# POOL writes its products into the mixed tile itself, and two buffers go

## The chip, the cores and the metric

The kernel runs on one core of a Trainium2 chip. The metric is the device time of one execution in microseconds (us). The core's engines are TensorE (PE, matrix products), VectorE (DVE), ScalarE (ACT), GpSimd (POOL) and SyncE (SP, which here issues the transfers). Each runs its own list of instructions in order; semaphores make one wait for another.

## The reference

Three layers stand behind each other: attention over keys near each query and over 24 block summaries, a channel mixer gated by a sigmoid, and a token and channel mixer. There are 2 sequences of 768 rows with 512 channels (8 heads of 64). The change is in the second layer:

```python
def _moe_ref(x, mu_k, mu_r, w_k, w_v, w_r) -> np.ndarray:
    B, S, D = x.shape
    x_prev = np.concatenate([np.zeros((B, 1, D), dtype=np.float32), x[:, :-1, :]], axis=1)
    xk = mu_k * x + (1.0 - mu_k) * x_prev
    xr = mu_r * x + (1.0 - mu_r) * x_prev
    k = np.maximum(xk @ w_k, 0.0)
    v = k * k @ w_v
    r = 1.0 / (1.0 + np.exp(-(xr @ w_r)))
    return (r * v).astype(np.float32)
```

Its input x is the attention's output. Each row is mixed with the row before it, once with the weights mu_k for the branch through w_k and w_v, and once with mu_r for the gate through w_r. The third layer follows on the result: `h = np.maximum(xt @ w_tok1, 0.0) @ w_tok2` over the tokens, then `(u + np.maximum(u @ w_ch1, 0.0) @ w_ch2)` over the channels.

## The kernel before, in words

**Numbers in two parts.** Matrix products of the second and third layer are made three times, from a high part and a low part of each operand (hi*hi, hi*lo, lo*hi; `mm3`, L432). ACT copies a tile to its high part, and POOL or DVE subtracts that from the tile for the low part.

**Attention.** 24 units (2 sequences, 6 tiles of 128 queries, 2 halves of the heads) go through scores on PE (sp, L303), mask and minimum on DVE (sm, L309), exponential on ACT (pe, L312), division by the sum on POOL (pe, L322), transposition on PE (pt, L328) with a copy to PT, the product with the values on PE (pv, L345), and a copy by ACT into xT (L350). xT holds the activations with the channels on the partitions. Block summaries are written by POOL into kw (L229).

**The mixed tiles.** `mixed` (L417 to L425) takes 256 rows and all 512 channels, in four slices of 128 channels (d). For each slice POOL multiplies the rows shifted by one with 1 - mu into a tile tmp (L421), from a tag with two buffers, and DVE adds mu times the rows and writes slice d of the tile xk (L422). xk has one buffer. When the four slices are done, ACT copies xk to the high part xh (L423) and DVE subtracts for the low part xl (L424); xh and xl have two buffers each. Six mixed tiles feed the branch (`main`), six the gate (`gate_pass`), and `main` makes one of the gate's tiles a second time, so that 13 are made: 52 products and 52 updates.

**The branch and the gate.** `main` makes, for each mixed tile, four groups of 24 matmuls into a bank ko. `k2_tile` squares the positive part: rl on ACT (L444) and DVE (L445), high part kh on ACT (L446), low part kl on POOL (L447). While the next group runs, the group before is multiplied with w_v into acc (12 matmuls). The gate's products go into ro (24 matmuls for each mixed tile), and a sigmoid on ACT and a product on DVE (L605) put them into ybuf. Then come h (L432, token mixing, 18 matmuls each), gh and gl (the two parts of its positive part, L660 and L661), ho, and the channel mixing (go and o).

**The weights.** They come in 64 bits; ACT, DVE (L145, L149, L155), ACT (high part w, L157) and POOL (low part w, L158) turn each block of 128 x 512 into two parts. Two wf buffers lie between DVE and POOL.

**The order.** The code is written as generators that hand out work in turns (`attention`, `main`, `gate_pass`, weights by credits). A scheduler then sets the order of each engine from estimated durations and priorities; some weight steps are kept in program order. So an edit in one place can move instructions on all engines. SP's list holds transfers only.

**What else uses the two buffers.** Three mask tiles are built at the start in the tag t32, the same tag as tmp.

Of the kernel before, what the change touches and what calls it, by code (L numbers as in the profile page):

```python
# [9 lines left out]
F32 = mybir.dt.float32  # L10
# [4 lines left out]
ALU = mybir.AluOpType  # L15
# [9 lines left out]
MW = 256  # L25
# [26 lines left out]
def fused_kernel(ctx, tc, q, k, v, vt, mu, w_k, w_v, w_r, w_t1, w_t2, w_c1, w_c2, out):  # L52
    nc = tc.nc
# [132 lines left out]
    work = pool("work", "left")  # L186
    xp = pool("xp", "left", reuse_waits="tile")
    XB = S + 1
    xT = xp.tile([128, KD, B * XB], F32, name="xT")
# [224 lines left out]
    def mixed(t0, mu, om):  # L414
        x0 = t0 // S * XB + 1 + t0 % S
        xk = work.tile([128, KD, MW], F32, tag="x32", bufs=1, name="xk")
        hi = work.tile([128, KD, MW], F32R, tag="xh", bufs=XBUFS, name="xh")  # L417
        lo = work.tile([128, KD, MW], F32R, tag="xl", bufs=XBUFS, name="xl")
        for d in range(KD):
            tmp = work.tile([128, MW], F32, tag="t32", bufs=2, name="tmp")  # L420
            nc.gpsimd.tensor_scalar(tmp, xT[:, d, x0 - 1:x0 - 1 + MW], om[:, d:d + 1], 1.0, ALU.mult, ALU.mult)  # L421
            nc.vector.scalar_tensor_tensor(xk[:, d], xT[:, d, x0:x0 + MW], mu[:, d:d + 1], tmp, ALU.mult, ALU.add)  # L422
        nc.scalar.copy(hi, xk)  # L423
        nc.vector.tensor_tensor(lo, xk, hi.bitcast(F32), ALU.subtract)  # L424
        return [(hi[:, d], lo[:, d]) for d in range(KD)]  # L425
# [29 lines left out]
    def make(c):  # L455
        if c not in made and c < NMC and done_tiles[0] >= (c + 1) * MT:
            made[c] = mixed(c * MW, muk, omk)
        elif c not in made and NMC <= c < 2 * NMC and c - NMC in done:
            made[c] = mixed((c - NMC) * MW, mur, omr)
# [73 lines left out]
    masks = []  # L533
    for kind in range(3):
        mc = const.tile([128, NC], F32, name=f"mask{kind}")
        mm = work.tile([128, 2, 128], F32, tag="t32", bufs=2, name="mm")
        for half in range(2):
            m = mm[:, half, :NC]
            nc.gpsimd.memset(m, 0.0)
            first = 64 * half - PAD  # L540
            keys = m[:, NB:NC] if half == 0 else m[:, 0:NK]
            for base, cm, st in ((first + EDGE, -1, 1), (EDGE - first, 1, -1)):
                nc.gpsimd.affine_select(out=keys, in_=keys, pattern=[[st, NK]], compare_op=ALU.is_ge, fill=-8.0 * BIG,
                                        base=base, channel_multiplier=cm)
            if kind == 1 and half == 0:
                nc.gpsimd.memset(m[:, NB:NB + PAD], -8.0 * BIG)
            if kind == 2 and half == 1:
                nc.gpsimd.memset(m[:, NK - PAD:NK], -8.0 * BIG)
            nc.gpsimd.memset(m[:, 0:NB] if half == 0 else m[:, NK:NC], math.sqrt(D) * math.log(BLOCK))
            nc.gpsimd.tensor_scalar(mc[64 * half:64 * half + 64], m[64 * half:64 * half + 64], 1.0, 1.0, ALU.mult, ALU.mult)  # L550
        masks.append(mc)
# [269 lines left out]
```

## Time and profile before

| | |
|---|---|
| three timed runs | 520.34, 521.74, 524.0 us; median 521.74 |
| the profiled execution | its span, from first to last instruction, is 518.7 us; its time beside the span is not given, so the median of the runs stands for it |
| busy time | PE 500.0, DVE 250.7, POOL 205.2, ACT 204.2 us |
| the chain that ended last | PE 80%, POOL 7%, issue 4%, DVE 3%, transfers 2%, ACT 2% |
| granted clock of PE, mean | 0.994 |

A matmul's busy time runs from its start to its modelled end, and successive ones overlap, so a busy PE can still be one that waits a little. The profile's names read "out<-in"; a bracket behind a row gives the idle time of that engine just before, and what ended it.

### The profile page before, as it was taken

How to read it: one execution, taken by the hardware profiler on the slowest of the kernel's cores; microseconds unless marked ns; L12 is line 12 of the kernel's file. 1: busy time of each engine (PE TensorE's matmuls, PEld its weight loads, DVE VectorE, ACT ScalarE, POOL GpSimd, SP SyncE). 2: the span in 40 equal slices, each digit the busy share in tenths (PEclk: the TensorE clock that was granted, in tenths of full speed). 3: DMA queues.
4: the chain of work that ended last, by engine and by line, in shares of the span. 5: the costliest groups of instructions: out<-in, count | busy, mean ns of one | idle time of the engine just before them, and what ended most of it. 6: DMA issues, size and time to landing. Idle time of an engine off the chain costs nothing.

```text
span 518.7 us, 7924 instructions
## 1 busy us (share of the span) xinstructions
PE 500.0 (96%) x2968; PEld 405.6 (78%) x2968; DVE 250.7 (48%) x556; ACT 204.2 (39%) x471; POOL 205.2 (40%) x298
## 2 busy tenths in 40 slices
PE   8997889999999999999999999999999999999995
PEld 3566767888789988888867788888888888888884
DVE  3869998551132667587656766443331211311112
ACT  0668669763342555446345344443211110100100
POOL 6579989972152665388523323322100000000000
PEclk9899999999999999999999999999999999999998
DMA  8999923210066000000176361000020000200002
GB/s 265 322 307 370 313 65 102 67 51 0 1 244 243 1 2 0 1 1 1 42 243 221 145 202 42 1 1 0 1 81 2 0 0 1 81 1 0 1 0 81
DMA packets 24197, 45.40 MB, mean 88 GB/s; under 512 B 2112, under 2 KB 11328, under 8 KB 24160
## 3 DMA queue, kind: packets, MB, share of 16 engines
q1 hardware_dynamic: 24160, 44.90, 26.7%
q8 instruction: 23, 0.38, 0.3%
q14 instruction: 14, 0.11, 0.1%
HBM read 41.16 MB, written 3.15 MB: 85 GB/s over the span
## 4 chain that ended last, share of the span: by engine, by line
PE 80%; POOL 7%; issue 4%; DVE 3%; DMA 2%; ACT 2%; SPq 1%; POOLq 0%; DVEq 0%; ACTq 0%
PE o L746 19%; PE go L432 19%; PE ko L432 11%; PE acc L432 10%; PE ro L432 5%; PE pv L345 3%; PE sp L303 3%; PE ho L432 3%; POOL pe L322 3%; PE h L432 2%; PE pt L328 2%; POOL w L158 2%; PE spin L511 2%; POOL tmp L421 1%; DMA xT<-in_vt_dram 1%
## 5 line engine op out<-in xcount | busy, mean ns | idle before, releaser
L432 PE MATMUL go<-u,w 128*128 128x512 f32 x432 | 106.6, 393 | 0.0
L158 POOL TENSOR_TENSOR w<-wf,w 128x512 fp32r<-128x512 f32 x50 | 65.9, 1320 | 76.9 <-ACT w L157 75.6
L432 PEld LDWEIGHTS go<-u,w 128*128 128x128 f32 x432 | 80.7, 188 | 17.6
L746 PE MATMUL o<-w,gh 128*128 128x512 f32 x288 | 89.0, 395 | 0.0
L661 DVE SCALAR_TENSOR_TENSOR gl<-go,gh 128x512 fp32r<-128x512 f32 x36 | 24.9, 691 | 121.1 <-ACT gh L660 120.9
L432 PE MATMUL ko<-xh,w 128*128 128x256 f32 x384 | 78.1, 289 | 1.6 <-ACT xh L423 0.8
L660 ACT ACTIVATE gh<-go 128x512 fp32r<-128x512 f32 x36 | 21.6, 599 | 128.7 <-PE go L432 128.7
L432 PEld LDWEIGHTS ko<-xh,w 128*128 128x128 f32 x384 | 61.8, 188 | 5.2 <-POOL w L158 1.2
L746 PEld LDWEIGHTS o<-w,gh 128*128 128x128 f32 x288 | 54.0, 188 | 12.0
L432 PE MATMUL acc<-w,kh 128*128 128x512 f32 x192 | 59.8, 401 | 0.7 <-ACT kh L446 0.6
L746 PE MATMUL o<-w,gl 128*128 128x512 f32 x144 | 55.4, 394 | 0.0
L432 PE MATMUL ko<-xl,w 128*128 128x256 f32 x192 | 54.8, 285 | 0.0
L322 POOL TENSOR_SCALAR pe<-pe,den 128x120 f32<-128x120 f32 x96 | 46.2, 499 | 6.7 <-DVE den L320 6.2
L157 ACT CAST w<-wf 128x512 fp32r<-128x512 f32 x50 | 30.9, 618 | 44.7 <-DVE wf L155 42.7
L447 POOL TENSOR_TENSOR kl<-rl,kh 128x512 fp32r<-128x512 f32 x24 | 34.6, 1443 | 34.8 <-ACT kh L446 32.6
L421 POOL TENSOR_SCALAR tmp<-xT,oms 128x256 f32<-128x256 f32 x52 | 34.0, 664 | 33.1 <-DVE xk L422 23.9
L155 DVE SCALAR_TENSOR_TENSOR wf<-wst,wf 128x512 int32<-128x512 int32 x50 | 43.3, 870 | 7.4 <-ACT wst L145 5.7
L312 ACT ACTIVATE pe<-sm,mn 128x120 f32<-128x120 f32 x96 | 37.0, 387 | 22.5 <-DVE mn L309 16.4
L445 DVE TENSOR_TENSOR rl<-rl 128x512 f32<-128x512 f32 x24 | 19.6, 818 | 46.2 <-ACT rl L444 46.2
L432 PEld LDWEIGHTS acc<-w,kh 128*128 128x128 f32 x192 | 34.3, 188 | 8.4 <-ACT kh L446 1.3
L432 PE MATMUL acc<-w,kl 128*128 128x512 f32 x96 | 36.5, 401 | 2.0 <-POOL kl L447 2.0
L422 DVE SCALAR_TENSOR_TENSOR xk<-xT,mus,tmp 128x256 f32<-128x256 f32 x52 | 35.7, 709 | 5.0 <-POOL tmp L421 5.0
(79 smaller groups left out, 722.5 us busy)
## 6 DMA issues: line engine op xcount, KB each, us to landing
wst<-in_moe_w_ch_dram SPq DMA_DIRECT2D x24, 512.0 KB
wst<-in_moe_w_k_dram SPq DMA_DIRECT2D x8, 512.0 KB
wst<-in_moe_w_v_dram SPq DMA_DIRECT2D x8, 512.0 KB
kw<-in_k_dram SPq DMA_DIRECT2D x12, 320.0 KB
wst<-in_moe_w_tok_dram SPq DMA_DIRECT2D x6, 512.0 KB
out_dram<-o SPq DMA_DIRECT2D x12, 256.0 KB
ybuf<-in_v_dram SPq DMA_DIRECT2D x12, 192.0 KB
vw<-in_v_dram SPq DMA_DIRECT2D x12, 192.0 KB
```

The costliest lines, as they stand in the source:

```text
L155: nc.vector.scalar_tensor_tensor(wi, top, 3, wi, ALU.logical_shift_left, ALU.bitwise_or)
L157: self.rounded.append(nc.scalar.copy(hi, wf))
L158: nc.gpsimd.tensor_tensor(lo, wf, hi.bitcast(F32), ALU.subtract)
L312: nc.scalar.activation(pe, s, AF.Exp, bias=mn[:, p:p + 1], scale=-1.0, accum_out=den[:, p:p + 1])
L322: nc.gpsimd.tensor_scalar(z["P"][p], z["P"][p], den[:, p:p + 1], 1.0, ALU.mult, ALU.mult)
L421: nc.gpsimd.tensor_scalar(tmp, xT[:, d, x0 - 1:x0 - 1 + MW], om[:, d:d + 1], 1.0, ALU.mult, ALU.mult)
L422: nc.vector.scalar_tensor_tensor(xk[:, d], xT[:, d, x0:x0 + MW], mu[:, d:d + 1], tmp, ALU.mult, ALU.add)
L432: nc.tensor.matmul(o, l, r, start=(first and i == 0), stop=(last and i == 3 * n - 1))
L447: nc.gpsimd.tensor_tensor(lo, rl, hi.bitcast(F32), ALU.subtract)
L660: nc.scalar.activation(hi, o, AF.Relu)
L661: nc.vector.scalar_tensor_tensor(lo, o, 0.0, hi.bitcast(F32), ALU.max, ALU.subtract)
L746: nc.tensor.matmul(acc[t], l, r, start=(f == 0 and i == 0), stop=(f == nf - 1 and i == 2))
```

## The change

POOL's product of slice d goes into slice d of xk, and DVE reads that slice and overwrites it. tmp is gone, and with it the two buffers of 256 columns; the masks are built in the tag rl, which has two larger buffers. The instructions are the same in number and shape. One line fewer moves the line numbers behind it by one.

```diff
@@ -417,9 +417,8 @@
         hi = work.tile([128, KD, MW], F32R, tag="xh", bufs=XBUFS, name="xh")
         lo = work.tile([128, KD, MW], F32R, tag="xl", bufs=XBUFS, name="xl")
         for d in range(KD):
-            tmp = work.tile([128, MW], F32, tag="t32", bufs=2, name="tmp")
-            nc.gpsimd.tensor_scalar(tmp, xT[:, d, x0 - 1:x0 - 1 + MW], om[:, d:d + 1], 1.0, ALU.mult, ALU.mult)
-            nc.vector.scalar_tensor_tensor(xk[:, d], xT[:, d, x0:x0 + MW], mu[:, d:d + 1], tmp, ALU.mult, ALU.add)
+            nc.gpsimd.tensor_scalar(xk[:, d], xT[:, d, x0 - 1:x0 - 1 + MW], om[:, d:d + 1], 1.0, ALU.mult, ALU.mult)
+            nc.vector.scalar_tensor_tensor(xk[:, d], xT[:, d, x0:x0 + MW], mu[:, d:d + 1], xk[:, d], ALU.mult, ALU.add)
         nc.scalar.copy(hi, xk)
         nc.vector.tensor_tensor(lo, xk, hi.bitcast(F32), ALU.subtract)
         return [(hi[:, d], lo[:, d]) for d in range(KD)]
@@ -533,7 +532,7 @@
     masks = []
     for kind in range(3):
         mc = const.tile([128, NC], F32, name=f"mask{kind}")
-        mm = work.tile([128, 2, 128], F32, tag="t32", bufs=2, name="mm")
+        mm = work.tile([128, 2, 128], F32, tag="rl", bufs=2, name="mm")
         for half in range(2):
             m = mm[:, half, :NC]
             nc.gpsimd.memset(m, 0.0)
```

The scheduler puts the instructions of PE, ACT, DVE and POOL in another order from the first mixed tile on; on SP two loads move. PE's last 945 of 2570 rows are the same. Three places follow.

On POOL, from the second mixed tile of the branch to the second kl, before:

```order
L158 TENSOR_TENSOR w<-wf,w 128x512
L421 TENSOR_SCALAR tmp<-xT,oms 128x256 x2
L322 TENSOR_SCALAR pe<-pe,den 128x120 x4
L158 TENSOR_TENSOR w<-wf,w 128x512
L421 TENSOR_SCALAR tmp<-xT,oms 128x256 x2
L158 TENSOR_TENSOR w<-wf,w 128x512
L322 TENSOR_SCALAR pe<-pe,den 128x120 x4
L447 TENSOR_TENSOR kl<-rl,kh 128x512
L158 TENSOR_TENSOR w<-wf,w 128x512
L229 TENSOR_SCALAR kw<-ks 128x4x24 x12
L158 TENSOR_TENSOR w<-wf,w 128x512
L447 TENSOR_TENSOR kl<-rl,kh 128x512
```

POOL at the same place now:

```order
L322 TENSOR_SCALAR pe<-pe,den 128x120 x4
L158 TENSOR_TENSOR w<-wf,w 128x512
L420 TENSOR_SCALAR xk<-xT,oms 128x256 x4
L322 TENSOR_SCALAR pe<-pe,den 128x120 x4
L158 TENSOR_TENSOR w<-wf,w 128x512
L446 TENSOR_TENSOR kl<-rl,kh 128x512
L158 TENSOR_TENSOR w<-wf,w 128x512
L229 TENSOR_SCALAR kw<-ks 128x4x24 x12
L446 TENSOR_TENSOR kl<-rl,kh 128x512
L158 TENSOR_TENSOR w<-wf,w 128x512 x3
```

The four products stand in one run; the first kl is behind the w that followed it, and the next w is ahead of the twelve kw.

On PE, where the first kl is used (the first acc of the branch, while the second sequence's attention begins; vp transposes the values' sums), before:

```order
L432 MATMUL acc<-w,kh 128x512 x4
L432 MATMUL acc<-w,kl 128x512 x2
L432 MATMUL acc<-w,kh 128x512 x2
L432 MATMUL acc<-w,kl 128x512
L432 MATMUL acc<-w,kh 128x512 x2
L432 MATMUL acc<-w,kl 128x512
L252 MATMUL vp<-ident,vrs 24x128
L328 MATMUL pt<-ident,pe 120x128 x4
L252 MATMUL vp<-ident,vrs 24x128
L303 MATMUL sp<-kw,qT 64x120 x15
L432 MATMUL ko<-xh,w 128x256
L432 MATMUL ko<-xl,w 128x256
```

PE at the same place now:

```order
L431 MATMUL acc<-w,kh 128x512 x4
L252 MATMUL vp<-ident,vrs 24x128
L328 MATMUL pt<-ident,pe 120x128 x4
L252 MATMUL vp<-ident,vrs 24x128
L431 MATMUL acc<-w,kl 128x512 x2
L431 MATMUL acc<-w,kh 128x512 x2
L431 MATMUL acc<-w,kl 128x512
L431 MATMUL acc<-w,kh 128x512 x2
L431 MATMUL acc<-w,kl 128x512
L431 MATMUL ko<-xh,w 128x256
L431 MATMUL ko<-xl,w 128x256
```

The vp and pt have moved ahead of the first acc with kl; the ko stand ahead of the sp.

On PE at the end of the gate: the last mixed tile's ro and the first two h, before:

```order
L432 MATMUL acc<-w,kl 128x512
L432 MATMUL ro<-w,xh 128x512 x4
L432 MATMUL h_3281<-y,w 128x512 x18
L432 MATMUL ro<-w,xl 128x512
L432 MATMUL ro<-w,xh 128x512 x2
L432 MATMUL ro<-w,xl 128x512
```

PE at the same place now, from the middle of the ro on:

```order
L431 MATMUL ro<-w,xh 128x512 x2
L431 MATMUL ro<-w,xl 128x512 x2
L431 MATMUL ro<-w,xh 128x512 x2
L431 MATMUL ro<-w,xl 128x512
L431 MATMUL ro<-w,xh 128x512 x2
L431 MATMUL ro<-w,xl 128x512
L431 MATMUL ro<-w,xh 128x512 x2
L431 MATMUL ro<-w,xl 128x512
L431 MATMUL h_3229<-y,w 128x512 x18
L431 MATMUL h_3261<-y,w 128x512 x18
```

Before, the 18 matmuls of the first h stood behind four of the ro; now all 24 ro stand together and both h behind them.

## Rows read from the trace of the kernel before

**Rows 1.** Busy us (and instructions) of PE, PEld, DVE, ACT, POOL by stage; clock, DMA.
```profile
40.00:75.00 35.00, 28.25 (x281) 23.09 (x277) 34.56 (x90) 23.57 (x71) 35.00 (x53) 1.00 0.83 265
75.00:263.00 188.00, 187.93 (x1330) 160.79 (x1329) 104.65 (x231) 97.66 (x222) 109.51 (x134) 1.00 0.17 57
263.00:290.00 27.00, 24.87 (x104) 18.94 (x103) 18.77 (x27) 12.64 (x22) 10.55 (x9) 1.00 0.72 266
290.00:519.00 229.00, 222.83 (x992) 181.82 (x991) 68.12 (x108) 50.73 (x87) 24.82 (x19) 0.99 0.08 28
```

**Rows 2.** Waits of PE in 35 to 80 us: total, times, longest.
```profile
PE pv L345 <- DVE PT L333: 3.7, 4, 1.3
PE acc L432 <- POOL kl L447: 1.4, 1, 1.4
```

**Rows 3.** Waits of PE in 185 to 312 us.
```profile
PE ho L432 <- DVE gl L661: 0.9, 1, 0.9
...
PE acc L432 <- POOL kl L447: 0.5, 1, 0.5
```

**Rows 4.** All waits of the execution, the one of tmp.
```profile
POOL tmp L421 <- DVE xk L422: 23.9, 15, 7.5
```

**Rows 5.** POOL in order of time: start, us, instruction, count, idle before.
```profile
39.98 0.94 POOL L421 TENSOR_SCALAR tmp<-xT,oms 128x256 f32<-128x256 f32 x2 [1.98 <-ACT xT L350]
...
53.98 1.91 POOL L421 TENSOR_SCALAR tmp<-xT,oms 128x256 f32<-128x256 f32 x2
...
64.71 1.28 POOL L447 TENSOR_TENSOR kl<-rl,kh 128x512 fp32r<-128x512 f32 x1
65.94 1.29 POOL L158 TENSOR_TENSOR w<-wf,w 128x512 fp32r<-128x512 f32 x1
67.21 4.88 POOL L229 TENSOR_SCALAR kw<-ks 128x96 f32<-128x96 f32 x12
72.06 1.27 POOL L158 TENSOR_TENSOR w<-wf,w 128x512 fp32r<-128x512 f32 x1
73.28 1.74 POOL L447 TENSOR_TENSOR kl<-rl,kh 128x512 fp32r<-128x512 f32 x1
```

**Rows 6.** PE in order of time, 35 to 80 us.
```profile
53.52 0.39 PE L432 MATMUL ko<-xh,w 128*128 128x256 f32 x1 [0.82 <-ACT xh L423]
...
66.04 0.72 PE L432 MATMUL acc<-w,kl 128*128 128x512 f32 x2 [1.42 <-POOL kl L447]
...
68.11 0.60 PE L328 MATMUL pt<-ident,pe 128*120 128x128 f32 x4
...
73.38 0.50 PE L432 MATMUL ko<-xh,w 128*128 128x256 f32 x2 [0.79 <-POOL w L158]
```

**Rows 7.** The chain that ended last: one group of the branch.
```profile
167.70 2.84 PE ko L432 x24
```

**Rows 8.** DVE, then POOL, then PE in order of time, 261 to 287 us.
```profile
261.06 1.23 DVE L424 TENSOR_TENSOR xl<-xk,xh 128x1024 fp32r<-128x1024 f32 x1 [3.54 <-ACT xh L423]
...
268.12 1.23 DVE L424 TENSOR_TENSOR xl<-xk,xh 128x1024 fp32r<-128x1024 f32 x1 [1.11 <-ACT xh L423]
...
263.98 0.64 POOL L421 TENSOR_SCALAR tmp<-xT,oms 128x256 f32<-128x256 f32 x1 [7.01 <-DVE xk L422]
264.59 1.28 POOL L447 TENSOR_TENSOR kl<-rl,kh 128x512 fp32r<-128x512 f32 x1
...
268.14 1.20 PE L432 MATMUL ro<-w,xh 128*128 128x512 f32 x4
269.19 4.36 PE L432 MATMUL h<-y,w 128*128 128x512 f32 x18
...
286.01 0.50 PE L432 MATMUL ho<-gl,w 128*128 128x512 f32 x1 [0.93 <-DVE gl L661]
```

**Rows 9.** POOL's busy time in the products alone (L421), 40 to 75 us.
```profile
40.00:75.00 35.00, 5.07 (x8) 1.00 0.83 265
```

## The prediction

> **What bounds the kernel now.** I read first the table of busy time by stage [rows 1], to find where TensorE (PE) stands idle at all. From 40 to 75 us PE is busy 28.25 of 35 us, while GpSimd (POOL) is busy 35.00 and VectorE (DVE) 34.56: this stage is set by POOL and DVE, and PE waits. From 75 to 263 PE is busy 187.93 of 188. In 263 to 290 it loses 2.13 us, and after 290 it is full up to the last output. The granted clock is 1.00 from 40 to 290, so the clock is no term. What the change can give back is thus PE idle time in two places, 6.75 and 2.13 us, some 8.9 us together or 1.7%; what it can cost has no such limit.
>
> The list of PE's waits says which of them end last there. In 35 to 80 us: PT from DVE 3.7 and one kl from POOL 1.4 [rows 2]; PE's own rows there add 0.8 for xh from ScalarE (ACT) and 0.8 for one w from POOL [rows 6]. In 185 to 312: gl 0.9, kl 0.5 [rows 3]. The largest wait that the change touches by name is another one: POOL's tmp waits 23.9 us for DVE's xk, 15 times, the longest 7.5 [rows 4]. That is POOL's time, and most of it lies where PE is full. So its going is worth nothing in itself; what counts is what POOL then does earlier or later for PE.
>
> **The change, part by part.** *Work.* Both programs issue 52 products and 52 updates of the same shape, and no other instruction is added or lost. The 8 products in 40 to 75 us take 5.07 us [rows 9], before and after. That an update reads and writes one tile I cost at nothing: DVE streams the same 256 columns. The two freed buffers hide no wait that I find. The masks' tile under the tag rl is used long before the first rl: nothing.
>
> *The wait.* Before, product d waited for update d-2 (two buffers), and so POOL came back four times to each mixed tile. Now product 0 waits for the tile xk to be free, that is for the subtraction xl of the mixed tile before, and products 1 to 3 follow without a wait. Queued behind that one wait on POOL are kl, w and pe; those who wait for these are PE's acc (kl), ko (w) and pt (pe). No row shows this wait. Below it is bounded by 0 (xl long done, as before 110 us, where each block stands several units after the last xl), above by the longest of the old kind, 7.5 [rows 4]. I take 0, since the old waits also ended with an xk that stood behind that same xl on DVE.
>
> *First stage, 40 to 75 us.* POOL's total work up to the second kl is the same set; its order is not. Three moves count. (a) The first kl, at 64.71 before, now stands behind the w that followed it at 65.94, which takes 1.29 [rows 5]: PE's acc, which waited for it until 66.04 [rows 6], comes 1.29 later. (b) PE has two vp and four pt moved ahead of that acc; the four pt cost 0.60 [rows 6], and fill that much of it. (c) The next w, at 72.06, stood behind the twelve kw (67.21, 4.88 us) and released PE's ko at 73.38 [rows 5, 6]; now it stands ahead of them, so this wait of 0.8 goes. What is late next is kw itself, 1.3 later, for which the 10 ko that now stand ahead of the sp are cover (24 of them take 2.84 [rows 7], so 10 take 1.2). The mixed tile is also done earlier, so PE's wait of 0.8 for xh at 53.52 [rows 6] goes, but it only brings PE sooner to the wait for kl: I count nothing. Sum: +1.29 - 0.60 - 0.8 = -0.1 us. Bounds: -3.0 if the waits for kl, xh and w all go (1.4 + 0.8 + 0.8), and +3.2 if nothing covers the kl (1.3) and the first two blocks of four each hold up the pe behind them by two products more, 0.94 a pair [rows 5]. I take the sum, near the middle, since POOL has no idle time here that the change could use.
>
> *75 to 263 us.* PE stands in another order until about 156 us, but is full before; with no idle time recorded, a gain is excluded. A loss begins where a kl or xh comes later than PE's cover. I take 0, and up to +6.5 for the range (five blocks that each hold the next pe or kl by two products of 0.65 [rows 8]).
>
> *263 to 290 us.* The last block of products waits for the xl that DVE does at 261.06 to 262.29, then takes about 4 x 0.65 = 2.6 and ends at 264.9; the last kl, at 264.59 before, stands behind it: +0.3 [rows 8]. PE now does all 24 ro of the last gate tile in one run and needs its xl (268.12 + 1.23 = 269.35) after four of them, which ended at 269.19: +0.2 [rows 8]. In return the gate's results come 4.4 us earlier to DVE, the 18 matmuls h that stood between, and the gl for which PE waited 0.9 at 286.01 [rows 3, 8] no longer stands behind their last multiplications on DVE: -0.9. Sum -0.4; bounds -1.4 (both waits of rows 3 go) and +1.3 (two products before the last kl, uncovered).
>
> Total -0.1 + 0 - 0.4 = **-0.5 us**. The profiled span is 518.7, the median of the three timed runs 521.74, so 3.0 us lie around the span; 518.2 + 3.0 gives **521.2 us**.
>
> **A rule that speaks against it.** A product alone on POOL takes 0.47 (two in 0.94 at 39.98), and two take 1.91 while DVE subtracts xl [rows 5]: the two engines hold each other up. The Trainium skill, page "SBUF — State Buffer", section "SBUF: two separate sides", says that a GpSimd operation and a VectorE operation with two SBUF inputs take one shared port pair in turn, for the whole instruction. The trace agrees with it at that row. By that rule a block of four meets an update after each product, and by it the sum would be that of the second rival below; by the measured 5.07 for 8 it is the -0.5 above.
>
> **The rivals.** *First, slower: the block holds POOL.* POOL runs in order. Where a block waits for xl with a kl right behind it, PE gets its kl late. PE's cover is the 24 ko of the next group, 2.84 us [rows 7]. With the longest old wait, 7.5 [rows 4], a place costs 7.5 - 2.84 = 4.7; two such places between 196 and 268, where a block stands before a kl four times, twice with a w or y between, give 521.7 + 9.3 = 531.0. It decides from a wait of 2.8 us in front of a kl. For it: POOL's xk chain already waits that long. Against it: then xh waits for the release of its two buffers by ro, which also holds the old products. *Second, the products stretch.* Eight products in blocks, each as slow as the two at 53.98 beside DVE (0.95 [rows 5]), take 7.6 in place of 5.07 [rows 9] on a POOL without idle time: +2.5 and the -0.5 of the sum, 523.7. For it, the row with 1.91; against it, most of the 8 before met updates too. *Third, faster: PE's idle time fills.* The first tile's four products are done by about 42 (39.98 + 4 x 0.47 [rows 5]), where PE's first ko came at 53.52 [rows 6]; its ko start some 4 us earlier and stand between the waits for PT. If two thirds of the 8.9 us go, it is 521.7 - 5.9 = 515.8. Against it: POOL and DVE stay full. *Fourth, nothing but the name of the wait changes:* the block waits for xl as long as tmp did, and PE sees none of it: 521.7.
>
> **How the numbers follow.** Forecast 0.60, first rival 0.14, second 0.10, third 0.09, fourth 0.07. The runs of before lie between 520.34 and 524.0, so about 1% (5.2 us) is what a measurement can tell from no change. The bounds of the terms make 521.7 - 4.4 = 517.3 and, with the first and last stage, 521.7 + 4.5 = 526.2; I leave out half of the third rival below and most of the first above: 516.8 to 526.8. Faster by over 1%: third rival and a little of the forecast, 0.10. Slower by over 1%: the first, and a little of the second, 0.16. Within 1%: 0.74.
>
> **What would show it.** Right: POOL's wait for xk is gone and small waits for xl stand in its place; POOL is still full in 40 to 75; the first ko starts before 50 us (53.5 before) and the first kl ends 1 to 1.5 us later; PE's wait for the w after kw is gone; the 24 ro stand together and the gl wait is under 0.5. The first rival shows as PE waiting for kl between 75 and 263; the second as products with a mean above 0.8 us in 40 to 75; the third as PE idle under 3 us there. I am wrong if the reordering of PE between 75 and 156 us, which I only bounded, opens a wait that no row of before hints at.

## The result, and the profile after

The kernel became slower. Before: 521.57 us, median of five runs (520.34 to 524.0). After: 527.77 us (525.77 to 535.84). The ratio is 1.0102, with a 95% interval of 1.0071 to 1.0133; when the changed kernel was timed again, it was 1.0132 (1.0096 to 1.0167). That is 5 to 7 us more where the forecast was -0.5, and 527.77 lies outside the range of 516.8 to 526.8. The first profile of the changed kernel fell into a disturbed execution, 535.84 us, so the rows of after come from a second one (e1 below), with a span of 526.0 us against 518.7.

The windows by stage of the changed kernel, with the columns and stages of [rows 1]:

```profile
40.00:75.00 35.00, 29.56 (x285) 24.58 (x281) 34.90 (x82) 21.42 (x61) 33.67 (x53) 0.95 0.88 274
75.00:263.00 188.00, 185.15 (x1284) 156.75 (x1283) 106.56 (x236) 97.91 (x227) 106.44 (x132) 0.98 0.16 52
263.00:290.00 27.00, 25.31 (x112) 20.41 (x111) 14.73 (x22) 12.62 (x21) 9.20 (x9) 0.94 0.70 239
290.00:519.00 229.00, 228.36 (x1016) 186.26 (x1015) 71.04 (x112) 52.98 (x91) 27.40 (x21) 1.00 0.08 30
```

Two columns have changed. PE's busy time from 75 to 263 us is 2.85 us short of the stage, where 0.07 was missing before. And the granted clock, 1.00 from 40 to 290 us before, is below 1.00 in three stages. Finer windows of the same kernel show where:

```profile
75.00:80.00 5.00, 5.00 (x48) 3.86 (x48) 4.90 (x13) 3.15 (x9) 3.37 (x3) 1.00 0.02 3
80.00:85.00 5.00, 3.44 (x35) 2.50 (x31) 4.55 (x21) 5.00 (x19) 3.42 (x5) 1.00 0.24 55
85.00:90.00 5.00, 4.04 (x25) 3.27 (x26) 4.31 (x12) 4.18 (x15) 5.00 (x8) 0.50 0.48 153
90.00:95.00 5.00, 5.00 (x45) 4.07 (x45) 5.00 (x19) 3.25 (x13) 5.00 (x7) 0.82 0.00 0
```

PE stands idle for 1.56 and 0.96 us, and then a granted clock of 0.50, which is 1.2 GHz in place of 2.4, follows from 85.0 to 91.8 us. Before, all four of these windows show 5.00 busy and 1.00. PE's timeline there (start, duration, in brackets the idle time just before):

```profile
81.40 0.28 PE L431 MATMUL ko<-xh,w 128*128 128x256 f32 x1
82.09 1.04 PE L303 MATMUL sp<-kw,qT 64*64 64x120 f32 x16 [0.42 <-DVE mn L309]
83.78 0.33 PE L328 MATMUL pt<-ident,pe 128*120 128x128 f32 x1 [0.64 <-POOL pe L322]
84.58 1.15 PE L328 MATMUL pt<-ident,pe 128*120 128x128 f32 x3 [0.48 <-POOL pe L322]
86.69 1.86 PE L303 MATMUL sp<-kw,qT 64*64 64x120 f32 x16 [0.96 <-PE pt L328]
```

Between two groups of ko PE has only attention: two units' sp and one unit's pt. The first sp and the pt wait for the softmax of a unit that is not through yet (mn on DVE, pe on POOL); for the last sp the profile names PE's own pt. The last sp takes 1.86 us for the same 16 records that took 1.04: that is the lower clock. These are the first units of the second sequence. Their softmax in the changed kernel, on DVE and then on POOL:

```profile
73.52 0.73 DVE L155 SCALAR_TENSOR_TENSOR wf<-wst,wf 128x512 int32<-128x512 int32 x1
74.17 1.50 DVE L149 TENSOR_SCALAR wf<-wst 128x512 int32<-128x512 int32 x1
75.59 0.68 DVE L333 COPY PT<-pt 120x512 f32<-120x512 f32 x1
76.19 1.17 DVE L155 SCALAR_TENSOR_TENSOR wf<-wst,wf 128x512 int32<-128x512 int32 x1
77.28 0.27 DVE L309 CUSTOM_DVE_ANT_0 sm<-sp,mask 128x120 f32<-128x120 f32 x1
```

```profile
67.96 1.28 POOL L158 TENSOR_TENSOR w<-wf,w 128x512 fp32r<-128x512 f32 x1 [1.33 <-ACT w L157]
69.23 4.48 POOL L229 TENSOR_SCALAR kw<-ks 128x96 f32<-128x96 f32 x12
...
83.10 2.11 POOL L322 TENSOR_SCALAR pe<-pe,den 128x120 f32<-128x120 f32 x4 [0.42 <-DVE den L320]
```

and the same first sm and first pe before:

```profile
72.24 0.28 DVE L309 CUSTOM_DVE_ANT_0 sm<-sp,mask 128x120 f32<-128x120 f32 x1
```

```profile
77.81 1.85 POOL L322 TENSOR_SCALAR pe<-pe,den 128x120 f32<-128x120 f32 x4 [1.22 <-DVE den L320]
```

The softmax starts 5.0 us later (72.24, now 77.28) behind weight steps, and its division on POOL 5.3 us later. The sp that it reads are later too. PE's rows of them now, and then before:

```profile
70.69 0.42 PE L303 MATMUL sp<-kw,qT 64*64 64x120 f32 x4
...
73.82 1.09 PE L303 MATMUL sp<-kw,qT 64*64 64x120 f32 x22
```

```profile
68.75 1.72 PE L303 MATMUL sp<-kw,qT 64*64 64x120 f32 x30
```

A record is a row of the trace; 32 of them make these sp. Four come at 70.69. The other 28 now stand behind a pt, a pv and four acc; before, all 32 stood ahead of those. On POOL kw begins at 69.23, against 67.21 before [rows 5], because POOL now waits 1.33 us for the w ahead of it. PE's longest waits from 30 to 330 us, which answer to [rows 2, 3]:

```profile
PE acc L431 <- POOL kl L446: 2.5, 3, 1.1
PE pv L345 <- ACT xT L350: 2.1, 1, 2.1
PE pt L328 <- POOL pe L322: 1.6, 3, 0.6
PE sp L303 <- PE pt L328: 1.0, 1, 1.0
```

The third place is the last block of products, where before kl was late by 0.5 [rows 3]; PE now waits longer, and the granted clock is 0.50 from 272.7 to 276.2 us:

```profile
270.10 1.20 PE L431 MATMUL acc<-w,kh 128*128 128x512 f32 x4 [0.57 <-ACT kh L445]
272.42 0.98 PE L431 MATMUL acc<-w,kl 128*128 128x512 f32 x2 [1.12 <-POOL kl L446]
```

**A balance.** In each slice of 5 us, let the idle time be 5 minus PE's busy time, and the clock's loss be the busy time times one minus the granted clock. Summed over stretches, idle + clock, in us:

| kernel | ratio to before, 95% interval | 40 to 75 | 75 to 105 | 105 to 260 | 260 to 325 |
|---|---|---|---|---|---|
| before | | 6.7 + 0.0 | 0.0 + 0.0 | 0.1 + 0.0 | 2.1 + 0.0 |
| changed (e1) | 1.0132 [1.0096, 1.0167] | 5.4 + 1.2 | 2.5 + 2.9 | 0.3 + 0.0 | 2.3 + 1.5 |
| e2 tmp, changed order | 1.0193 [1.0154, 1.0232] | 6.7 + 1.3 | 2.5 + 2.9 | 0.3 + 0.0 | 2.3 + 1.4 |
| e3 in place, old order, POOL free | 1.0058 [1.0029, 1.0086] | 5.9 + 3.2 | 0.4 + 0.0 | 0.0 + 1.8 | 2.6 + 1.7 |
| e4 in place, old order, two xk | 1.0001 [0.9971, 1.0031] | 6.9 + 0.0 | 0.8 + 0.0 | 0.0 + 0.0 | 2.0 + 0.0 |
| e5 changed, softmax first | 1.0145 [1.0101, 1.0189] | 6.5 + 1.3 | 1.1 + 5.0 | 0.3 + 0.0 | 2.3 + 0.0 |
| e6 old, one piece changed | 1.0111 [1.0077, 1.0146] | 6.8 + 0.0 | 1.4 + 6.3 | 0.1 + 0.0 | 2.1 + 0.0 |
| e7 changed, gaps filled | 1.0106 [1.0069, 1.0143] | 6.5 + 1.3 | 1.2 + 0.0 | 0.3 + 0.0 | 2.3 + 1.3 |
| e8 changed, third wf | 1.0111 [1.0081, 1.0142] | 2.8 + 6.6 | 3.7 + 2.7 | 0.0 + 0.0 | 2.3 + 0.0 |
| e9 changed, piece undone | 1.0176 [1.0140, 1.0212] | 6.5 + 1.7 | 3.0 + 1.7 | 0.3 + 0.0 | 2.3 + 0.0 |
| e10 old, PE's half of the piece | 1.0197 [1.0160, 1.0235] | 10.7 + 1.4 | 2.2 + 3.0 | 0.1 + 0.0 | 2.1 + 0.0 |
| e11 old, kw late alone | 1.0063 [1.0035, 1.0090] | 8.8 + 1.4 | 0.0 + 1.7 | 0.1 + 0.0 | 2.1 + 0.0 |
| e12 old, changed stretch | 1.0259 [1.0226, 1.0292] | 8.3 + 1.2 | 4.7 + 6.6 | 0.1 + 0.5 | 2.1 + 0.0 |
| e13 old, changed start | 1.0091 [1.0055, 1.0127] | 5.9 + 6.8 | 0.0 + 1.0 | 0.1 + 0.0 | 2.1 + 0.0 |
| e14 changed, old start | 1.0152 [1.0111, 1.0194] | 6.9 + 0.0 | 1.6 + 3.0 | 0.3 + 0.0 | 2.3 + 0.0 |

For the changed kernel these sums are 7.2 us above those of before, against 7.3 of the spans: 5.4 from 75 to 105, 1.7 from 260 to 325, 0.2 between them and -0.1 from 40 to 75. By the sums 1.6 of the 7.2 is idle time and 5.6 the clock.

Four things limit what the table tells. The sums don't fit every run so well: from the same sm (34.55 us before) to the same gh (457.58 before), e7's profile loses 6.3 us where its sums make 4.0, and e8's 6.5 where they make 9.2, so a term can be off by 2 to 3 us. The stretches are times, not parts of the program: e4's execution stands 7.3 us behind at that sm, and its 0.8 from 75 to 105 is the wait of 0.79 for w that before has at 73.38 [rows 6]. The split into idle and clock is not one by cause: where the clock is lower, PE can be busy in time that it would else wait, as e6 and e7 show below. And the ratio is from the timed runs, the sums from one profiled execution each; those of e9 and e14 were faster than their medians (527.52 of 530.54, and 526.7 of 528.97), those of e4 and e6 slower (527.43 of 522.14, and 532.02 of 527.36).

### The profile page after: what moved, and what is told of

It reads as the page before. It is cut to its first block, busy times and chain, and to the rows that moved or that the text cites. A ratio compares the mean times of both kernels' runs of the same rounds, so it can differ in the third digit from the quotient of the medians.

```text
span 534.0 us, 7892 instructions
## 1 busy us (share of the span) xinstructions
PE 510.9 (96%) x2968; PEld 412.8 (77%) x2968; DVE 253.7 (48%) x556; ACT 205.1 (38%) x471; POOL 201.8 (38%) x298
## 4 chain that ended last, share of the span: by engine, by line
PE 83%; DVE 9%; DMA 2%; issue 2%; SPq 1%; ACT 1%; POOL 1%; ACTq 0%; DVEq 0%; POOLq 0%
PE o L745 19%; PE go L431 19%; PE ko L431 12%; PE acc L431 11%; PE ro L431 6%; PE sp L303 4%; PE pv L345 3%; PE ho L431 3%; PE h L431 2%; PE pt L328 2%; DMA xT<-in_vt_dram 2%; DVE wf L155 2%; PE spin L510 2%; DVE wf L149 1%; PE utr L699 1%
## 5 line engine op out<-in xcount | busy, mean ns | idle before, releaser
L158 POOL TENSOR_TENSOR w<-wf,w 128x512 fp32r<-128x512 f32 x50 | 67.1, 1344 | 81.9 <-ACT w L157 81.9
L431 PE MATMUL ko<-xh,w 128*128 128x256 f32 x384 | 79.3, 292 | 0.3 <-POOL w L158 0.3
L431 PEld LDWEIGHTS ko<-xh,w 128*128 128x128 f32 x384 | 63.2, 193 | 3.3 <-issue 0.9
L431 PE MATMUL acc<-w,kh 128*128 128x512 f32 x192 | 61.0, 404 | 0.6 <-ACT kh L445 0.6
L155 DVE SCALAR_TENSOR_TENSOR wf<-wst,wf 128x512 int32<-128x512 int32 x50 | 48.5, 972 | 8.3 <-ACT wst L145 6.4
L322 POOL TENSOR_SCALAR pe<-pe,den 128x120 f32<-128x120 f32 x96 | 43.4, 471 | 20.6 <-DVE den L320 20.6
L431 PE MATMUL acc<-w,kl 128*128 128x512 f32 x96 | 37.6, 405 | 2.5 <-POOL kl L446 2.5
L420 POOL TENSOR_SCALAR xk<-xT,oms 128x256 f32<-128x256 f32 x52 | 32.6, 643 | 17.4 <-DVE xl L423 15.4
L421 DVE SCALAR_TENSOR_TENSOR xk<-xT,mus,xk 128x256 f32<-128x256 f32 x52 | 36.9, 749 | 3.8 <-POOL xk L420 3.8
L431 PEld LDWEIGHTS ko<-xl,w 128*128 128x128 f32 x192 | 37.0, 193 | 1.7 <-DVE xl L423 0.6
```

The lines of the kernel that those rows point to most:

```text
L155: nc.vector.scalar_tensor_tensor(wi, top, 3, wi, ALU.logical_shift_left, ALU.bitwise_or)
L158: nc.gpsimd.tensor_tensor(lo, wf, hi.bitcast(F32), ALU.subtract)
L322: nc.gpsimd.tensor_scalar(z["P"][p], z["P"][p], den[:, p:p + 1], 1.0, ALU.mult, ALU.mult)
L420: nc.gpsimd.tensor_scalar(xk[:, d], xT[:, d, x0 - 1:x0 - 1 + MW], om[:, d:d + 1], 1.0, ALU.mult, ALU.mult)
L431: nc.tensor.matmul(o, l, r, start=(first and i == 0), stop=(last and i == 3 * n - 1))
```

## The experiments

**How an order is set.** Most experiments put an engine's instructions in a given order with edges that order but don't wait. ORDER holds, for each engine, the positions that another kernel's instructions have (QUIET names the kinds that are left where they are):

```diff
+    def in_order_of(table):
+        for name, rs in table.items():
+            of = [i for i in nc.cur_bb.bb.instructions
+                  if str(i.engine).endswith(name) and type(i).__name__ not in QUIET and (name != "SP" or "DMA" in type(i).__name__)]
+            seq = [k for a, n in rs for k in range(a, a + n)]
...
+            for a, b in zip(seq, seq[1:]):
+                tc.add_manual_dep(of[b], of[a].name,
+                                  mybir.DependencyInfo(mybir.DependencyClass.NoSync, mybir.DependencyReason.DATA), reason="queue order")
+
+    in_order_of(ORDER)
```

**e1, the changed kernel again.** No edit.

> The changed kernel once more, for a profile that can be laid beside the one of before. In the profile at hand PE stands between 89.3 and 96.4 us with sp, pt and sp alone (idle 0.43, 0.64, 0.48 and 1.10 us before them) and the granted clock is 0.84 in 90 to 95 and 0.50 in 95 to 100. Theory A (the order that the scheduler gives the attention of the second sequence costs the time): the same stall and the same drop of the clock stand in this profile too, some 5 to 6 us together, and the time is 526 to 529. Theory B (the loss is spread, each block of four products holds POOL a little): no single stretch loses more than 2 us of PE time against before, and PE's waits for kl and pe are spread over 75 to 290.

527.84 us, and the stall and the drop of the clock stand at the same instructions, 5.4 us together. Theory A's condition holds; theory B's (no stretch over 2 us) doesn't.

**e2, the kernel before in the changed order.** It keeps tmp and its two buffers, and nothing is written in place:

```diff
+ORDER = order of the changed kernel, on PE, DVE, ACT, POOL and SP
```

> The kernel before, with its tmp tiles and two buffers, but with the instructions of all five engines put in the order of the changed kernel. Nothing is written in place. Theory A (the order costs): as slow as the changed kernel or a little slower, 526 to 532, with the stall on PE near 90 to 95 us. Rival (the place written to costs: an update that reads and writes one tile, or the wait for the tile to be free): near the kernel before, 520 to 523.

531.88 us, and from 75 to 105 the same 2.5 + 2.9. The order costs, with nothing written in place. By the ratios it costs rather more than in e1, though the two intervals touch; POOL's tmp still waits for xk here, 21.4 us in all.

**e3 and e4, in place in the old order.** In e3 POOL is left to the scheduler, which makes blocks of four products. In e4 all five engines stand in the old order. In the old order the first product of a mixed tile stands ahead of the xl of the tile before from the fourth tile on, so with one xk each would wait for the other (argued, not run); with two xk it doesn't, and kw gives a buffer for it:

```diff
-KB = 7
+KB = 6
...
-        xk = work.tile([128, KD, MW], F32, tag="x32", bufs=1, name="xk")
+        xk = work.tile([128, KD, MW], F32, tag="x32", bufs=2, name="xk")
```

> The changed kernel with PE, DVE, ACT and SP in the order of the kernel before; POOL's order is left to the scheduler, and its products stand in blocks of four. Theory A (the order of PE and DVE costs): 519 to 524, no stall on PE near 90 us and a granted clock of 1.00 there. Rival (the block of products on POOL or the writing in place costs): 526 to 530, with PE waiting for pe or kl behind a block of products.

> The changed kernel with two buffers for xk (and six instead of seven for kw, to make the room), and with all five engines in the order of the kernel before: the products are written in place, and no block waits for xl. Theory A: 519 to 524. Rival (writing in place itself makes products or updates longer): the mean of an update over 0.70 us and 524 to 530; that the two engines hold each other up more would show as products over 0.70 us.

523.91 and 522.14 us. e4 is level with before: the products in place cost nothing that can be measured. Its profile agrees row by row: the sm at 34.55 us before stands 7.3 us later, from a start that lost more to the clock, and the gh at 457.58 stands 6.8 later. e3 keeps the stretch from 75 to 105 nearly full (0.4); its 0.6% stand elsewhere, as 3.2, 1.8 and 1.7 us of the clock from 40 to 75, 105 to 260 and after 260. So about half of a loss of this size (0.58 of 1.02 to 1.32%) can come with one buffer and blocks of four even in the old order; the loss from 75 to 105 does not. This is the window of e4:

```profile
75.00:105.00 30.00, 29.22 (x298) 23.14 (x297) 26.71 (x97) 24.02 (x79) 28.26 (x45) 1.00 0.26 67
```

**e5, the late softmax moved ahead.** The changed order, with these rows moved (DVE is shown; pe moves in the same way on ACT and POOL):

```diff
 L155 wf
+L309 sm x4, the first unit
 L149 wf
 L333 PT
+L309 sm x4, L319 and L320 den, the second and the first unit
 L155 wf
-L309 sm x4, the first unit
...
```

> The changed kernel in its own order on all engines, but with the softmax of the first two units of the second sequence (8 sm, their pe, den and division) moved ahead of the weight steps that stand before them on DVE, ACT and POOL, and the last sm of the third unit ahead of the first update of the mixed tile. In the changed kernel's profile the first of these sm stands at 77.28 us, the first pe on POOL at 83.10, and PE waits 2.50 us between 81.7 and 86.7; the granted clock is 0.50 in 85 to 90 and 0.82 in 90 to 95. Theory A1 (that one late softmax is the loss): PE waits less than 0.6 us between 79 and 96, the clock stays at 1.00 there, and the time is 520.5 to 523.5. Rival A2 (the new order loses in many places, or the weight steps that are now later make PE wait for w instead): 525 to 528.

528.0 us: theory A1 falls, and the time is that of rival A2. The waits for pe are gone, but a wait of ko for w from POOL stands in their place, and the clock falls just the same. Nor were the weight steps all of the softmax's delay: moved ahead of them, the first sm still waits 1.49 us for sp and starts at 75.70, 3.5 us later than before. PE's timeline and the windows:

```profile
82.48 0.50 PE L431 MATMUL ko<-xh,w 128*128 128x256 f32 x2 [1.02 <-POOL w L158]
```

```profile
80.00:85.00 5.00, 3.98 (x36) 3.39 (x38) 1.73 (x6) 5.00 (x15) 3.87 (x6) 0.83 0.17 39
85.00:90.00 5.00, 5.00 (x37) 4.05 (x34) 4.97 (x17) 4.18 (x16) 5.00 (x7) 0.50 0.57 163
90.00:95.00 5.00, 5.00 (x40) 4.26 (x41) 5.00 (x18) 3.45 (x12) 5.00 (x6) 0.64 0.02 9
```

One wait of 1.02 us is followed by 10 us at or near 1.2 GHz, in which sp, pt and ko take turns. Idle time fell from 2.5 to 1.1, the clock's loss rose from 2.9 to 5.0.

**e6, one piece of the changed order in the old one.** The piece holds what the prediction priced as step (c) and its cover, and on PE it holds more: all of PE's rows from the first acc with kl to the pv behind the second acc (66 to 80 us before) stand in the changed order. In records of the traces:

```diff
 PE
+vp, pt x4, vp
 acc x8 (with kl and kh)
-vp, pt x4, vp
-sp x30
 ko x2
-sp x2, acc x4 (with kh), vp x2
 ko x10
+sp x4
 pt x4, pv x16
+acc x4 (with kh), sp x22, vp x2, sp x6
 acc x5
+pv x16
 acc x3, sp x16
-pv x16
 POOL
+w
 kw x12
-w
```

> The kernel before in its own order on all engines, but with one piece of the changed order: on PE the ten ko stand ahead of the first sp of the second sequence, and on POOL the w stands ahead of the twelve kw. DVE and ACT keep the old order, in which the first softmax of the second sequence stands ahead of two weight steps. Theory A1a (the step that the prediction priced at nothing, kw and sp later with ten ko as cover, is the loss): 523.5 to 528, with a stall on PE between 76 and 92. Theory A1b (the loss comes from DVE and ACT, where the softmax stands behind weight steps): 520 to 523.

527.36 us: 6.2 us for this piece, as much as the whole change. The cover (the work that PE has while an operand is on its way) fails in this way:

```profile
74.10 0.50 PE L432 MATMUL ko<-xh,w 128*128 128x256 f32 x2 [1.04 <-POOL w L158]
...
77.31 1.11 PE L328 MATMUL pt<-ident,pe 128*120 128x128 f32 x4 [1.41 <-DVE PT L333]
```

```profile
75.00:80.00 5.00, 3.59 (x28) 2.89 (x27) 2.25 (x3) 0.25 (x1) 3.70 (x12) 0.65 0.00 0
80.00:85.00 5.00, 5.00 (x35) 3.32 (x35) 0.85 (x9) 0.25 (x1) 0.00 (x0) 0.50 0.00 0
```

In 80 to 85 DVE, ACT and POOL have next to nothing to do: they wait for sp from a PE at 1.2 GHz, the first sm 6.90 us. This execution was the longest of the six, 532.02 us, and the drop is not what the piece needs in order to cost: two runs with a mean granted clock of 0.996, which leaves some 2 us for the clock in the whole execution, took 525.1 and 526.53 us, and a run of before at 0.996, timed with them, 521.18.

**e7, the gaps filled.** The changed order with seven small matmuls in the gaps (14 records in the trace):

```diff
         pt = bank("pt", 2, [128, NP, 128], "pt")
+        for _ in range({(1, 0, 0): 4, (1, 0, 1): 3}.get(z["u"], 0)):
+            nc.tensor.matmul(pt[:, NP - 1], ident, ident, start=True, stop=True)
```

> The changed kernel in its own order with seven small matmuls added that compute nothing of use (128 columns, into a bank that the transposes overwrite): one ahead of the sp at 82.09, three ahead of the pt at 83.78 and three ahead of the sp at 86.69, where PE stands idle 0.42, 0.64 and 0.96 us. Nothing that PE waits for comes earlier. If the drop of the clock follows the idle time: the granted clock stays at 1.00 in 85 to 95 and the time is 523.5 to 525.5, some 3 us under the changed kernel. If it does not follow it: 527 to 529.

```profile
85.00:90.00 5.00, 3.78 (x35) 2.85 (x33) 3.98 (x13) 4.19 (x17) 5.00 (x8) 1.00 0.49 157
90.00:95.00 5.00, 5.00 (x50) 4.07 (x49) 5.00 (x17) 3.42 (x12) 5.00 (x7) 1.00 0.11 13
```

The clock stays at 1.00 although 1.2 us of idle time is left (0.43 for sp, 0.78 for w). In five of the six runs the mean granted clock is 0.992 to 0.994, against 0.980 to 0.989 in the six of e1. In these runs the drop follows the gaps. The time is 526.37 us, 1.5 under e1 and less than the 3 expected; the intervals of the two ratios overlap. PE's rows in e7, then in e1, say why it is less:

```profile
87.06 1.04 PE L303 MATMUL sp<-kw,qT 64*64 64x120 f32 x16 [0.43 <-issue]
...
89.31 0.50 PE L433 MATMUL ko<-xh,w 128*128 128x256 f32 x2 [0.78 <-POOL w L158]
```

```profile
89.07 0.66 PE L431 MATMUL ko<-xh,w 128*128 128x256 f32 x2
```

e7's execution is 0.4 us behind e1's at 35 us and still at this sp (87.06 and 86.69). At the full clock PE then waits 0.78 us for w, which at the lower clock had come when PE was ready for it. Only behind that does e7 get ahead, by 0.9 us (an sp at 92.53 and 93.41). So the drop that the balance puts at 2.9 us cost 1.3 in these two profiles. The times agree: at a mean granted clock of 0.992 to 0.994 e7 takes 525.29 to 527.5 us, and runs of before timed with it take 521.88 to 524.32. Some 3 us of the loss need no drop of the clock.

**e8, a third wf.** The changed kernel, with the room of tmp given to wf:

```diff
-WF = 2
+WF = 3
```

> The changed kernel with the room of the two tmp buffers given to a third buffer for wf; the scheduler makes another order again. If the old order was a lucky one among many and any new order loses some us: 524 to 530. If the third buffer lets DVE run ahead of POOL in the first stage, where PE stands idle 5.4 us between 40 and 75: 516 to 520, and then this is a version faster than both.

527.24 us. PE's idle time from 40 to 75 falls from 5.4 to 2.8, and the clock takes 6.6 there. No version came out that beats before.

**e9 to e11, the piece taken out, and in halves.** e9 is the changed order with the two edits of e6 reversed (all of its PE rows, and POOL; the other engines free). e10 and e11 are e6 with its PE half and its POOL half alone, so e10 too moves more than the ten ko.

> The changed kernel with the piece of the sixth experiment undone, on PE and POOL in their changed order otherwise: the first sp of the second sequence stand ahead of the ten ko again, and the twelve kw ahead of the w; DVE, ACT and SP are left to the scheduler. So far the profiles lose, between 75 and 105 us, to idle PE and to the clock: before 0.0, changed 2.5 and 2.9, the old order with the piece 1.4 and 6.3. If the piece is the cause: under 1.5 us lost between 75 and 105, and 521 to 524.5 (what the changed kernel loses after 260 us, 1.7 more than before, stays). If it only is one of several ways into the same loss: 525.5 to 529, with idle time and a drop of the clock at another place between 75 and 105.

> The kernel before in its own order, with half of the piece: on PE the ten ko stand ahead of the sp, and on POOL the w stays behind the twelve kw. ko then waits for that w, some 73.4 us in the profile of before. If sp behind ko is what costs: the softmax of the second sequence starts late as in the sixth experiment, 524 to 529. If the late kw is what costs: 520.5 to 523.

> The kernel before in its own order, with the other half: on POOL the w stands ahead of the twelve kw, and PE keeps its order, in which the first sp stand ahead of the ko. POOL waits for that w (1.33 idle and 1.28 of work in the changed kernel), so kw and sp come some 2 us later. If the late kw is what costs: 523.5 to 528. If sp behind ko is what costs: 520.5 to 523.5, PE's wait for w (0.8) being gone and some 2 us of waiting for kw in its place.

530.54, 531.35 and 524.78 us. The wait that stands out in each, from 75 to 105 in e9, from 40 to 105 in the others:

```profile
PE ko L431 <- POOL w L158: 3.7, 2, 2.2
```

```profile
PE ko L432 <- POOL w L158: 5.1, 1, 5.1
```

```profile
PE sp L303 <- POOL kw L229: 2.7, 1, 2.7
```

e9 goes against the piece as the cause in the changed kernel: with it out, ko waits for w, and the time is above both ranges that were expected. Whoever is served first on POOL, kw or w, the other is late. PE's half cost more than the late kw, but each half alone also makes a wait that the other would have covered.

**e12 to e14, stretch and start.** The changed order on PE, DVE, ACT and POOL in a part of the old one, and the reverse:

```diff
 e12: before, its tmp, old order
+changed order from the second group of ko (66 us) to the first units of the second sequence (86 us)
 e13: before, its tmp, old order
+changed order from the first mixed tile (40 us) to where e12 begins
 e14: the changed kernel
+old order from the first mixed tile to where e12 begins
```

> The kernel before, with tmp and two buffers, in its own order, but with the changed order on PE, DVE, ACT and POOL in one stretch: from the second group of ko (PE waits there for the first kl, 66 us in the profile of before) to the first units of the second sequence (some 86 us). Theory W (the loss is made in this stretch, where attention, weights and kw meet): 524.5 to 529, with 3 us or more lost between 75 and 105 to idle PE and the clock. Rival F (it is made ahead of it, in the first stage): 520 to 523.

> The kernel before in its own order, but with the changed order on PE, DVE, ACT and POOL from the first mixed tile (40 us) up to where the stretch of the twelfth run begins. Theory W: 520 to 523. Rival F: 524 to 529, with the changed kernel's new wait of PE there (pv for xT from ACT, 2.1) and a drop of the clock behind it. Rival S (each order fits only with its own continuation): here and in the next run over 525.

> The changed kernel, in place, in its own order, but with the order of the kernel before on PE, DVE, ACT and POOL from 40 us up to where the stretch of the twelfth run begins. Theory W: 525 to 529, the loss between 75 and 105 stays. Rival F: 520 to 523.5. Rival S: over 525, with the loss at another place than in the changed kernel.

535.06, 526.77 and 528.97 us. The windows of e12, of e13 and of e14:

```profile
75.00:105.00 30.00, 25.31 (x207) 19.16 (x206) 24.39 (x83) 18.77 (x62) 22.02 (x32) 0.73 0.18 51
```

```profile
40.00:75.00 35.00, 29.13 (x234) 24.18 (x235) 31.44 (x79) 21.38 (x62) 26.80 (x42) 0.79 0.87 271
```

```profile
75.00:105.00 30.00, 28.44 (x248) 22.09 (x246) 20.16 (x85) 22.26 (x77) 25.50 (x38) 0.89 0.18 52
```

The loss of 75 to 105 goes with the changed order of the stretch: 11.3 us with it and the old start (e12), 4.6 with it in place and the old start (e14), 1.0 without it (e13). So theory W holds for that loss. Rival F's time came true in e13 by another way: the clock takes 6.8 us, at 0.50 from 46.3 to 56.6 and from 70.2 to 77.1, behind waits of at most 1.6 us; the wait of pv for xT is 0.7. By the times rival S holds in part: all three are over 525, but e14 loses at the place where the changed kernel does. Why the stretch costs 11.3 in e12 and 4.6 in e14 stays open; the two differ in tmp and in what follows.

## Why the prediction was wrong

**The step that failed** is the middle term, "75 to 263 us: 0", with its reason "PE stands in another order until about 156 us, but is full before", and the sentence on which all terms rest, "the granted clock is 1.00 from 40 to 290, so the clock is no term". Measured by the balance: +5.6 from 75 to 260 (2.7 idle, 2.9 clock). The prediction had bounded this term by +6.5 but left it out of the range: 526.2 is 521.7 with the +3.2 of the first stage and the +1.3 of the last alone. That PE was full told what it had to do before, and nothing of how close behind its work the next operand was. The list of waits before could not show it either: a wait that is just covered leaves no row. The sign that was there, and was priced at a cover of 1.2 us, is step (c): kw behind w, ten ko ahead of sp. The cover was meant for kw alone, and kw made no wait; but all the softmax of the next units stood behind those sp, 5.0 us later, and PE's cover was used up when they came due. The price of step (c) also left out that a pt, a pv and four acc had moved ahead of 28 of the 32 sp records. e6 prices these moves, with the w ahead of kw, at 6.2 us in the old order. In the changed order they are one of two ways into the same loss: e5 and e9 relieve the softmax and then ko waits for w. The clock was no term in the prediction, and its drop does add to the loss, but by e7 some 1.3 us and not 2.9. What is shown (e2, e4, e12, e14) is that the order of the stretch makes the loss and the place of the product doesn't; no single move in it has been shown to be the cause.

**First stage**, forecast -0.1: -0.1 by the balance, with other parts, so that the agreement is luck. The first kl releases PE at 66.69 against 66.04 [rows 6], +0.65 where 1.29 - 0.60 was forecast; the wait for the w behind kw fell from 0.8 to 0.24; the first ko came at 48.67, before 50, as forecast. Not foreseen: pv waits 2.1 for xT once, and behind it the clock takes 1.2. POOL, forecast to stay full, is busy 33.67 of 35 us.

**Last stage**, forecast -0.4: +1.7. PE waits 1.1 for the last kl behind the block of products where it waited 0.5, so +0.6 (forecast +0.3), the gl wait went from 0.9 to 0.6 (forecast 0), no wait for xl shows behind the first four ro (forecast +0.2), and the clock takes 1.5 behind the kl, which was no term.

**The wait for xk.** On POOL 15.4 us, four times, the longest 5.9, in place of 23.9 [rows 4]; the prediction took it at 0. PE has no new wait for kl between 75 and 263 longer than 0.3. The first rival had the right sign and the wrong mechanism.

**The second rival** falls: the eight products take 4.91 us against 5.07 [rows 9]. An update in place does take longer at the median, and not at the least (min/median/max ns; first changed, then before):

```profile
L421 DVE SCALAR_TENSOR_TENSOR xk<-xT,mus,xk x52: 454/694/1517, 42.7 to 271.2; 128x256 f32<-128x256 f32 x52
```

```profile
L422 DVE SCALAR_TENSOR_TENSOR xk<-xT,mus,tmp x52: 450/484/1511, 42.9 to 266.5; 128x256 f32<-128x256 f32 x52
```

All 52 take 36.9 us against 35.7, 1.2 us of DVE, which e4 bears as well (692 at the median) without loss. The Trainium skill's page "SBUF — State Buffer", section "SBUF: two separate sides", has GpSimd and two-operand VectorE work take turns at a port; an update beside the next product of its block, at an unchanged least duration, agrees with that.

## What to carry to other kernels

Where a scheduler orders the code, an edit is two edits, and they are told apart by running the old code in the new order (e2) and the new code in the old order (e4); here the edit in the old order, with room for a second xk, was worth 0.0%, and the new order alone 1.9%. A full engine is not a safe one: before pricing a reordering at zero, ask of each operand that now comes later how long it stood ready before, and follow the whole chain behind it, not the first wait. A bound that was worked out for a term belongs in the range. And a wait on TensorE in a stretch of small matmuls can bring a drop of the granted clock, which belongs in the range too; but idle time and clock in a profile don't say what each is worth. With the drop gone, 1.3 of its 2.9 us came back, because other waits took its place (e7).

## What was not expected of the hardware

The clock does not follow idle time alone. From 40 to 75 us before, 6.7 us idle left the granted clock at 1.00; one wait of 1.02 us in e5 was followed by ten microseconds at 0.50 (83.3 to 93.6). The same waits (0.57 us for kh, then 1.12 for kl) at the same instructions near 270 us were followed by a drop in the changed kernel and by none in e5, whose order there is the same. Windows of the changed kernel, then of e5:

```profile
272.00:274.00 2.00, 1.58 (x4) 1.30 (x5) 0.89 (x2) 1.32 (x2) 0.36 (x1) 0.69 0.38 156
```

```profile
272.00:274.00 2.00, 0.88 (x5) 0.54 (x4) 1.61 (x2) 0.36 (x1) 1.33 (x1) 1.00 0.92 344
```

And from 10 to 40 us, where before, the changed kernel and e4 have the same instructions in the same order, the clock took 1.5, 0.0 and 8.3 us of their profiled executions. A single profile can thus carry several microseconds that are no property of the kernel; the ratios above are from the timed runs for that reason.
